# A conditioned transformer block on one core: GpSimd's place among VectorE's work, memory products in 32-row blocks, and where the last x load stands

## The chip, the cores and the metric

The kernel runs on one core of a Trainium2 chip. Its engines are TensorE (PE), VectorE (DVE), ScalarE (ACT), GpSimd (POOL) and SyncE (SP, which here only gives out transfers). Each engine runs its own list of instructions in order and waits on semaphores for the others. The metric is the device time of one execution in microseconds; the median of several runs counts.

## What is computed

One token block of 2048 rows and 448 features goes through a layer norm, an attention with a compressive memory, a second layer norm and a gated feed-forward layer. Shift, scale and gate vectors come from a condition `c`. Everything is bf16 outside.

```python
mod = silu(c) @ w_mod                        # sa, ca, ga, sb, cb, gb: six vectors of 448
h = layernorm(x) * (1 + ca) + sa
x = x + ga * A(h)
h = layernorm(x) * (1 + cb) + sb
x = x + gb * B(h)

# A: 16 heads of 28; 4 segments of 512 rows, M and z start at zero
phi = lambda t: where(t > 0, t + 1, exp(t))
for s in range(4):
    p = softmax(q_s k_s^T * scale + causal_mask)       # the causal mask stays within the segment
    a_mem = (phi(q_s) @ M) / (phi(q_s) . z + 1e-6)
    o_s = g * a_mem + (1 - g) * (p @ v_s)              # g = sigmoid(beta), one for each head
    M = M + phi(k_s)^T v_s ;  z = z + sum(phi(k_s))
A = concat(o_s) @ wo
# B
B = (sigmoid(h @ w_gate) * (h @ w_up)) @ w_down        # inner width 1792
```

## The kernel before

The 2048 rows are four segments of 512, each of four tiles of 128. The 16 heads are four groups of four; a head takes 32 partitions (`HP`), 28 of them data (`Dh`), so that one group fills 128. The column behind a head's 28 values of v is one, so that z comes as a column of M. All weights stay in SBUF after one load.

The code doesn't issue instructions directly. It builds a graph of nodes with `add`; a node names an engine (or several, of which the planner chooses one), a planned duration in ns, a function that writes its instructions, the nodes it depends on, the buffers it takes (`take`, `use`), and a priority. `Graph.run` (L207) then simulates the engines in time: whenever an engine is free it gives it the ready node with the highest rank plus priority. The numbers in `PRM` are those priorities, one for each node of a kind. On TensorE a change of `mode` costs `SWITCH` and staying gains `STAY`. A node with `lock=True` is a VectorE operation that the planner keeps apart from GpSimd's: in planned time a GpSimd node doesn't start before the last locked VectorE node has ended (`held`), and a locked VectorE node doesn't start while GpSimd is busy (`shut`). At the end (L287 to L289) the nodes' functions are called in planned order. Semaphores come afterwards from what the instructions read and write, in the order in which they were written out; each engine's list follows that order too. The planned times themselves leave nothing on the chip.

The order of stages: loads, layer norm and projections of segment 0 (`ln1`, `turned`, `proj`), then for every segment attention in two halves of two head groups (`attention`, `unit`), `memory` for the next segment, the output product and the second layer norm (`wo_ln2`), and `ffn`. The planner mixes all of this. Segments 0 and 1 turn normalised rows on TensorE (L745); the other layer norms turn them by transposing transfers on the Sync queue (L690).

What the change and the prediction touch:
- `load` (L422) puts one transfer on the Sync queue (`nc.sync`) or on ScalarE's; `load_x` (L458) loads tiles of x. L654 loads tiles 12 to 15; L655 loads the down weights in four pieces; L652 loads the gate weights through ScalarE's queue.
- `wz` (L494) is the last tile of `x_sb`, index 15, set to zero by VectorE at the start. ScalarE's fills (L511) read it, and so do the dummy products (L1058): 16 nodes of two products each, whose result nobody reads. Their priority is far below everything else, so that they fill TensorE's idle time in the plan.
- `W_p` (L641) copies the q and k weights into padded form; the projection products are L805 (q, k) and L817 (v).
- `memory` (L836): phi of k (L830 to L833), a transposing transfer (L841), four products of 128 x 128 for each head group (L847), an update of `M_sb` on VectorE (L854, L856), and a copy times the block mask `bmask` on VectorE or GpSimd (L860), which sets to zero what mixes different heads.
- `unit` (L930): the masked exponentials times v (L938), and for segments 1 to 3 phi of q times the masked memory in one full product (L949).
- GpSimd also does the layer norms' `rstd` (L559, L560), part of the causal masks (L910), of the weight scalings (L681) and of the modulations (L702).

Of the kernel before, what the change touches and what calls it, by code (L numbers as in the profile page):

```python
# [7 lines left out]
BF16 = mybir.dt.bfloat16  # L8
# [7 lines left out]
SWITCH = 96  # L16
# [29 lines left out]
    "mask": (1420295, 2300886, 1661567, 1988009, 1742158, 1915688, 1601937, 2188133, 1494944, 1748413, 1621429,  # L46
# [16 lines left out]
    "mem": (-214050, -174920, 501877, -265144, 92656, -155063, -11188, -639908, -57241, 71005, -88187, -198959, 48359,  # L63
# [68 lines left out]
class Graph:  # L132
# [74 lines left out]
    def run(self):  # L207
# [12 lines left out]
        while done < len(self.nodes):  # L220
            moved = False
            for e in ENGINES:
                if at[e] > t or (e == "POOL" and held > t):
                    continue
# [879 lines left out]
```

## Time and profile before

| | us |
|---|---|
| median of 3 runs | 297.54 |
| lowest and highest run | 293.26, 298.44 |
| the profiled execution | 292.1 |
| its span, first to last instruction | 290.4 |
| PE busy in the span | 245.0 (84%) |
| DVE busy | 203.7 (70%) |
| ACT busy | 152.8 (53%) |
| POOL busy | 62.4 (21%) |

An engine's busy time counts its instructions, not its waits. PEld is the load of weights into TensorE, which runs beside products. A row of a timeline merges instructions of one line that follow each other; the idle time before the first of them stands in brackets, with what ended it. PEclk is TensorE's granted clock as a share of 2.4 GHz, so 0.50 is the lower level, 1.2 GHz.

### The profile page before, as it was taken

Reading aid. Unit: us, or ns where it says so; the run is one execution under the profiler, and the core shown is the slowest. Engines: PE = TensorE matmul, PEld = TensorE weight load, DVE = VectorE, ACT = ScalarE, POOL = GpSimd, SP = SyncE. Lnnn points to the kernel's source line nnn. Section 1 sums busy time; section 2 is a strip of 40 time slices with the busy share of each in tenths; the row PEclk is TensorE's granted clock in tenths of the full one; section 3 lists DMA queues with packets and bytes.
Section 4 is the critical chain, followed back from the end, with each engine's and each line's share of the span. In section 5 each row is a group of like instructions: output and inputs, shape, how many; then the busy total and the mean of one; then the engine's idle time right before and its main releaser. Section 6 shows DMA issues by size and latency. Waiting matters only on the chain. (4 is left out here: it accounts for less than half of the span.)

```text
span 290.4 us, 5584 instructions
## 1 busy us (share of the span) xinstructions
PE 245.0 (84%) x2185; PEld 108.0 (37%) x2185; DVE 203.7 (70%) x472; ACT 152.8 (53%) x186; POOL 62.4 (21%) x119
## 2 busy tenths in 40 slices
PE   8800089987598696998899999998999999999995
PEld 3600033533233232344355433443444434443442
DVE  5490006999989998899974999996989944414331
ACT  4220008879678966786645867776752133213210
POOL 7021000322506705057500200351010400000000
PEclk9955579999689977799999999999999999999999
DMA  7999976414330332000550011013210043000001
GB/s 198 218 225 223 216 227 141 83 38 91 84 72 3 82 73 64 18 2 18 78 116 2 18 52 33 2 33 47 59 34 0 3 87 81 16 18 16 19 16 47
DMA packets 32102, 20.73 MB, mean 71 GB/s; under 512 B 20491, under 2 KB 30412, under 8 KB 32076
## 3 DMA queue, kind: packets, MB, share of 16 engines
q1 hardware_dynamic: 29868, 17.11, 26.9%
q10 hardware_dynamic: 2208, 3.27, 5.3%
q8 instruction: 17, 0.28, 0.4%
q14 instruction: 9, 0.07, 0.1%
HBM read 11.07 MB, written 1.84 MB: 44 GB/s over the span
## 5 line engine op out<-in xcount | busy, mean ns | idle before, releaser
L1023 PE MATMUL ps<-hT,wgu 64*128 64x512 bf16 x784 | 96.3, 383 | 3.8 <-DVE fT L1030 1.5
L1028 ACT ACTIVATE tt<-ps 128x512 f32<-128x512 f32 x56 | 33.4, 596 | 63.8 <-PE ps L1023 61.9
L897 ACT ACTIVATE pT<-ps 128x2048 bf16<-128x2048 f32 x32 | 60.1, 1878 | 9.7 <-PE ps L883 8.8
L1030 DVE SCALAR_TENSOR_TENSOR fT<-tt,ps 128x512 bf16<-128x512 f32 x56 | 38.0, 681 | 34.5 <-ACT tt L1028 34.5
L1023 PEld LDWEIGHTS <-wgu 64*128 64x128 bf16 x784 | 39.7, 95 | 52.9 <-issue 17.6
L1042 PE MATMUL ps<-wd_sb,fT 128*128 128x448 bf16 x224 | 46.8, 353 | 0.0
L910 POOL TENSOR_SCALAR_AFFINE_SELECT pT<-pT 128x512 bf16<-128x512 bf16 x24 | 15.9, 673 | 74.8 <-ACT pT L897 58.7
L1058 PE MATMUL ps<-x_sb 128*128 128x448 bf16 x32 | 10.3, 495 | 24.3 <-DMA x_sb<-in_A_x_dram 23.1
L805 PE MATMUL ps<-hT,wqk 64*128 64x512 bf16 x224 | 28.9, 395 | 1.0 <-ACT pT L897 1.0
L1042 PEld LDWEIGHTS <-fT 128*128 128x128 bf16 x224 | 20.4, 98 | 23.6 <-issue 7.0
L788 ACT CAST kT<-ps 128x512 bf16<-128x512 f32 x11 | 6.5, 587 | 29.6 <-PE ps L805 29.4
L552 DVE BATCH_NORM_STATS2 st<-x_sb 128x6 f32<-128x448 bf16 x32 | 19.5, 611 | 1.5 <-DMA x_sb<-in_A_x_dram 1.1
L790 DVE CAST kT<-ps 128x512 bf16<-128x512 f32 x5 | 3.4, 675 | 24.6 <-PE ps L805 24.6
L883 PE MATMUL ps<-qT,kT 28*128 28x512 bf16 (+3 forms) x256 | 17.0, 312 | 3.5 <-ACT pT L903 1.5
L805 PEld LDWEIGHTS <-wqk 64*128 64x128 bf16 x224 | 11.6, 98 | 15.8 <-issue 6.2
L913 DVE TENSOR_TENSOR pT<-pT,cmask 128x512 bf16<-128x512 bf16 x40 | 17.0, 450 | 0.5 <-ACT pT L897 0.5
L903 ACT ACTIVATE pT<-ps 128x2048 bf16<-128x2048 f32 x8 | 15.0, 1881 | 3.6 <-PE ps L883 3.6
L560 POOL TENSOR_TENSOR rs<-rs,mhalf 128x1 f32<-128x1 f32 (+1 forms) x26 | 15.9, 613 | 2.2
L1001 PE MATMUL ps<-wo_sb,oT 128*128 128x448 bf16 x64 | 13.6, 353 | 1.5 <-DVE kT L790 1.2
L817 PE MATMUL ps<-wvv,hT 64*128 64x448 bf16 x112 | 13.3, 365 | 1.7 <-DVE vt L790 1.5
L559 POOL TENSOR_SCALAR rs<-mv 128x1 f32<-128x1 f32 (+1 forms) x26 | 6.2, 238 | 39.7 <-DVE mv L553 36.9
L938 PE MATMUL ps<-pT,vt 128*32 128x512 bf16 (+3 forms) x256 | 12.7, 315 | 2.3 <-DVE pT L913 1.7
(96 smaller groups left out, 273.4 us busy)
## 6 DMA issues: line engine op xcount, KB each, us to landing
out_dram<-ot SPq DMA_DIRECT2D x16, 112.0 KB, 1.7
hT<-hT SPq DMA_DIRECT2D x6, 256.0 KB, 3.2
hT<-hT SPq DMA_DIRECT2D x6, 192.0 KB, 2.7
x_sb<-in_A_x_dram SPq DMA_DIRECT2D x2, 448.0 KB, 13.5
wgu<-in_B_w_up_dram SPq DMA_DIRECT2D x1, 896.0 KB, 11.2
wd_sb<-in_B_w_down_dram SPq DMA_DIRECT2D x2, 448.0 KB, 9.5
wgu<-in_B_w_gate_dram ACTq DMA_DIRECT2D x1, 896.0 KB, 7.3
fT<-in_w_mod_dram SPq DMA_DIRECT2D x2, 392.0 KB, 13.0
```

Source lines behind the costliest of these rows:

```text
L552: nc.vector.bn_stats(st_r[:, st.at, :], src)
L560: nc.gpsimd.tensor_tensor(r, r, mhalf[:, 0:w], ALU.pow)
L805: nc.tensor.matmul(pf(b), lhsT=w, rhs=piece(hT, i, half), start=(i == 0), stop=(i == NP - 1))
L883: nc.tensor.matmul(ps[:, lg.at + hs, o:o + nq], lhsT=kT_r[r, k.at, hcs[u], kb * P:(kb + 1) * P], rhs=qT_r[r, q.at, hcs[u], kb * P:L], star ...
L897: nc.scalar.activation(pT_r[:, pTs[units[0]].at, :, w0:w0 + L], ps_, AF.Exp, scale=scale)
L903: nc.scalar.activation(dst, ps_.rearrange("p h (u w) -> p u h w", u=2), AF.Exp, scale=scale)
L910: nc.gpsimd.affine_select(out=blk, in_=blk, compare_op=ALU.is_ge, fill=0.0, base=0, pattern=[[0, 4], [1, P]], channel_multiplier=-1)
L913: nc.vector.tensor_tensor(blk, blk, cmask[:].rearrange("p (o k) -> p o k", o=1).to_broadcast([P, 4, P]), ALU.mult)
L1023: nc.tensor.matmul(pf(b), lhsT=wgu[half * HR:(half + 1) * HR, chunk_of(i, half), fs], rhs=piece(hT, i, half), start=(i == 0), stop=(i == N ...
L1028: a = act(485, lambda gp=gp, tt=tt: nc.scalar.activation(tt_r[:, tt.at, :], pf(gp), AF.Tanh, scale=0.5), [n], use=[gp, tt], prio=pr("tanh" ...
L1030: f = dve(597, lambda up=up, tt=tt, ft=ft: nc.vector.scalar_tensor_tensor(fT_r[:, ft.at, :], tt_r[:, tt.at, :], 1.0, pf(up), op0=ALU.add, ...
L1042: nc.tensor.matmul(pf(b)[:, 0:D], lhsT=fT_r[:, fts[fc].at, t * P:(t + 1) * P], rhs=wd_sb[:, fc, :], start=(fc == 0), stop=(fc == NFC - 1))
```

## The change

Three things change in the code, and the planner's numbers with them.

- In the plan a GpSimd node may start no earlier than 175 ns (`BEHIND`) after the start of the last VectorE node. When the instructions are written out, the first instruction of each GpSimd node gets a semaphore wait on the last VectorE instruction whose planned end lies at or ahead of the GpSimd node's planned start.
- The memory is kept as blocks of 32 rows and 32 columns for each head, `M_sb` being 128 x 32 for a head group instead of 128 x 128. The update takes 16 small products for a head group, the read four small ones; `bmask` goes, a column `rmask` takes its place, and the copy runs on VectorE alone.
- The dummy products are defined ahead of the loads, and the load of tiles 12 to 15 depends on the last dummy and on ScalarE's fills.
- `SWITCH` is 164 ns from mode H to mode R and 96 for all other changes (96 for all before); `STAY`, `COST` and all numbers of `PRM` are new, so that the order of the nodes differs throughout.

```diff
-SWITCH = 96
+SWITCH = {("H", "R"): 164}
+OTHER = 96
+BEHIND = 175
...
-STAY = 25968
-COST = {"ACT": 0.86, "DVE": 1.009, "POOL": 0.81}
+STAY = 151782
+COST = {"ACT": 1.037, "DVE": 1.012, "POOL": 0.764}
...
-                if at[e] > t or (e == "POOL" and held > t):
+                if at[e] > t or (e == "POOL" and max(held, gate) > t):
...
-                    if e == "DVE" and n.lock:
-                        held = n.end
+                    if e == "DVE":
+                        gate = t + BEHIND
+                        if n.lock:
+                            held = n.end
...
+        block = tc.nc.cur_bb.bb.instructions
+        last = []
         for n in order:
-            if n.fn is not None:
-                n.fn(n.eng) if len(n.durs) > 1 else n.fn()
+            if n.fn is None:
+                continue
+            was = len(block)
+            n.fn(n.eng) if len(n.durs) > 1 else n.fn()
+            if n.eng == "DVE":
+                last.append((n.end, block[-1].name))
+            elif n.eng == "POOL":
+                before = [name for end, name in last if end <= n.start]
+                if before:
+                    tc.add_manual_dep(block[was], before[-1], mybir.DependencyInfo(
+                        mybir.DependencyClass.Sync, mybir.DependencyReason.DATA), reason="place among VectorE's work")
...
-    M_sb = const.tile([P, NHC, P], F32, name="M_sb")
+    M_sb = const.tile([P, NHC, HP], F32, name="M_sb")
...
-    rm_r = ring("rm", 5, [P, P], BF16)
+    rm_r = ring("rm", 5, [P, HP], BF16)
...
+    n_warm = None
+    for i in range(NWARM):
+        n_warm = add("PE", 740 if i < 7 else 380, warm_fn, [n_wz, n_warm], prio=-4 * BIG if i else 2 * BIG, mode="F", take=() if i else [b_w],
+            use=[b_w] if i else ())
...
-    load_x("SP", 3 * TPS, 4 * TPS, first(18), 41)
+    load_x("SP", 3 * TPS, 4 * TPS, first(18), 41, [n_warm, n_pads, *n_vpad, *n_vone, *n_opad])
...
         nc.vector.tensor_reduce(epsc[:], eps4[:], axis=mybir.AxisListType.X, op=ALU.add)
+        nc.vector.tensor_reduce(rmask[:], rsel[:], axis=mybir.AxisListType.X, op=ALU.add)
...
                 for kb in range(TPS):
-                    nc.tensor.matmul(pf(b)[:, 0:P], lhsT=pk_r[:, pk.at, kb, :],
-                                     rhs=vt_r[:, vt_of[s].at, kb, hc * 4:(hc + 1) * 4, :].rearrange("p h e -> p (h e)"),
-                                     start=(kb == 0), stop=(kb == TPS - 1))
+                    for hs in range(4):
+                        r = slice(hs * HP, (hs + 1) * HP)
+                        nc.tensor.matmul(pf(b)[r, 0:HP], lhsT=pk_r[:, pk.at, kb, r], rhs=vt_r[:, vt_of[s].at, kb, hc * 4 + hs, :],
+                                         start=(kb == 0), stop=(kb == TPS - 1), tile_position=(0, HP * hs),
+                                         skip_group_check=True)
...
-                    nc.vector.tensor_tensor(M_sb[:, hc, :], M_sb[:, hc, :], pf(b)[:, 0:P], ALU.add)
-            u = dve(197, up, [m, M_n.get((s, hc))], use=[b], prio=pr("mem", s))
+                    nc.vector.tensor_tensor(M_sb[:, hc, :], M_sb[:, hc, :], pf(b)[:, 0:HP], ALU.add)
+            u = dve(110, up, [m, M_n.get((s, hc))], use=[b], prio=pr("mem", s))
...
-            rm_n[(s + 1, hc)] = shared((200, 430), lambda e, hc=hc, rm=rm: vec(e).tensor_tensor(
-                rm_r[:, rm.at, :], M_sb[:, hc, :], bmask[:], ALU.mult), [u, n_masks], take=[rm], prio=pr("mem", s))
+            rm_n[(s + 1, hc)] = dve(110, lambda hc=hc, rm=rm: nc.vector.tensor_scalar(
+                rm_r[:, rm.at, :], M_sb[:, hc, :], rmask[:, 0:1], None, op0=ALU.mult), [u, n_coef], take=[rm],
+                prio=pr("mem", s), lock=True)
...
-            m = add("PE", 220, lambda: nc.tensor.matmul(pf(mem), lhsT=rm_r[:, rm.at, :], rhs=pq_r[:, pq.at, :],
-                                                        start=True, stop=True),
-                    [f, rm_n[(s, hc)]], take=[mem], use=[pq, rm], mode="F", prio=pr("phi", s))
+
+            def read():
+                for hs in range(4):
+                    r = slice(hs * HP, (hs + 1) * HP)
+                    nc.tensor.matmul(pf(mem)[r, :], lhsT=rm_r[r, rm.at, :], rhs=pq_r[r, pq.at, :], start=True, stop=True,
+                                     tile_position=(HP * hs, HP * hs), skip_group_check=True)
+            m = add("PE", 235, read, [f, rm_n[(s, hc)]], take=[mem], use=[pq, rm], mode="D", prio=pr("phi", s))
```

The masks' set-up on GpSimd loses `bmask` and gains one small selection for `rsel`; both kinds of edits that stand above as "..." follow from these.

## Rows read from the trace of the kernel before

**Rows 1.** The profile page: span and instructions.

```profile
span 290.4 us, 5584 instructions
```

**Rows 2.** Timeline, TensorE, 0 to 48: start, us, engine, line, operation, tiles, count, idle.

```profile
5.56 3.25 PE L1058 MATMUL ps<-x_sb 128*128 128x448 bf16 x14
...
11.44 3.06 PE L745 MATMUL ps<-ident,xn 128*128 128x128 bf16 x32
37.61 3.14 PE L1058 MATMUL ps<-x_sb 128*128 128x448 bf16 x8 [23.10 <-DMA x_sb<-in_A_x_dram]
40.68 3.63 PE L805 MATMUL ps<-hT,wqk 64*128 64x512 bf16 x32
```

**Rows 3.** The same timeline's VectorE and ScalarE, 0 to 52.

```profile
16.87 1.63 DVE L640 COPY wqk<-wd_sb 64x784 bf16<-64x784 bf16 x4
...
16.09 1.45 ACT L767 ACTIVATE hT<-ps,cols 128x512 bf16<-128x512 bf16 x2 [1.56 <-DVE hT L765]
...
44.69 0.60 ACTq L425 DMA_DIRECT2D wgu<-in_B_w_gate_dram  x1
```

**Rows 4.** The same timeline's Sync queue, 0 to 48 and 40 to 100.

```profile
24.47 0.55 SPq L425 DMA_DIRECT2D x_sb<-in_A_x_dram  x1
25.08 10.68 SPq L425 DMA_DIRECT2D wd_sb<-in_B_w_down_dram  x4
...
61.69 2.60 SPq L841 DMA_TRANSPOSE pk<-pq  x2
```

**Rows 5.** Windows: stretch, its us, busy us of each engine (instructions), clock, DMA.

```profile
14.50:37.60 23.10, 0.00 (x1) 0.00 (x0) 6.74 (x18) 1.48 (x3) 3.09 (x8) 0.50 1.09 229
...
50.00:150.00 100.00, 84.67 (x836) 36.35 (x830) 93.60 (x226) 77.22 (x89) 38.73 (x57) 0.91 0.30 60
150.00:210.00 60.00, 58.30 (x553) 26.32 (x550) 50.45 (x117) 42.41 (x45) 9.61 (x18) 1.00 0.16 32
210.00:290.40 80.40, 77.13 (x585) 33.32 (x581) 41.55 (x78) 20.91 (x33) 4.52 (x10) 1.00 0.11 30
```

**Rows 6.** DMA issues by line: tiles, queue, count, KB each, median us to landing.

```profile
wgu<-in_B_w_gate_dram ACTq DMA_DIRECT2D x1, 896.0 KB, 7.3
...
wd_sb<-in_B_w_down_dram SPq DMA_DIRECT2D x2, 448.0 KB, 9.5
...
pk<-pq SPq DMA_TRANSPOSE x12, 2.4
```

**Rows 7.** GpSimd and VectorE at 97, then lines (busy, mean) and lines (min/median/max).

```profile
97.27 3.07 POOL L681 TENSOR_TENSOR wd_sb<-wd_sb,rep 128x448 bf16<-128x448 bf16 x3
...
97.73 3.06 DVE L565 TENSOR_SCALAR xn<-x_sb,mv,rs 128x448 bf16<-128x448 bf16 x4
...
L565 DVE TENSOR_SCALAR xn<-x_sb,mv,rs 128x448 bf16<-128x448 bf16 x32 | 13.7, 465 | 0.5 <-POOL rs L560 0.5
...
L831 DVE TENSOR_SCALAR e<-qT 128x512 bf16<-128x512 bf16 x12 | 5.2, 435 | 0.0
...
L565 DVE TENSOR_SCALAR xn<-x_sb,mv,rs x32: 354/391/1100, 7.5 to 232.3; 128x448 bf16<-128x448 bf16 x32
L831 DVE TENSOR_SCALAR e<-qT x12: 260/286/1116, 87.3 to 206.6; 128x512 bf16<-128x512 bf16 x12
```

**Rows 8.** Small products (timeline, lines) and the memory's copies (lines).

```profile
68.50 0.40 PE L847 MATMUL ps<-vt,pk 128*128 128x128 bf16 x4
...
9.65 1.93 PE L604 MATMUL ps<-silu,pT 112*128 112x1 bf16 x62 [0.82 <-DMA pT<-in_w_mod_dram]
44.24 0.39 PE L883 MATMUL ps<-qT,kT 28*128 28x512 bf16 x4
...
L847 PE MATMUL ps<-vt,pk x48: 218/219/230, 68.5 to 174.3; 128*128 128x128 bf16 x48
...
L949 PE MATMUL ps<-pq,rm 128*128 128x512 bf16 x12 | 4.3, 402 | 0.5 <-DVE pq L833 0.5
L856 DVE TENSOR_TENSOR M_sb<-M_sb,ps 128x128 f32<-128x128 f32 x8 | 2.2, 277 | 1.4 <-PE ps L847 1.4
```

More of the change, by code (lines that the diff above doesn't have):

```diff
@@ L22 @@
 PRM = {
[23 rows of a table removed]
-    "mask": (1420295, 2300886, 1661567, 1988009, 1742158, 1915688, 1601937, 2188133, 1494944, 1748413, 1621429,
[16 rows of a table removed]
-    "mem": (-214050, -174920, 501877, -265144, 92656, -155063, -11188, -639908, -57241, 71005, -88187, -198959, 48359,
[22 rows of a table removed]
-    "tanh": (518834, 901538, 371356, 312956, 429296, 1610358, 1231833, 455336, 658639, 1233093, 953232, 1034923,
[16 rows of a table removed]
-    "phi": (92371, 88481, 47667, 108382, -497773, 32202, 492785, 282150, 660225, 55845, -9786, 163048, 345946, 155916,
[3 rows of a table removed]
-}
-STAY = 25968
-COST = {"ACT": 0.86, "DVE": 1.009, "POOL": 0.81}
[23 rows of a table added]
+    "mask": (1520615, 1413694, 1279386, 2003105, 1818148, 1973568, 1670422, 2469718, 1732752, 2449207, 2306151,
[16 rows of a table added]
+    "mem": (-185723, 115729, 59349, 101126, -27425, -125584, 150803, 226014, 77645, 95180, -386111, -12099, 159007,
[22 rows of a table added]
+    "tanh": (1916179, 1874612, 1112957, 1758741, 1844683, 2214238, 1662134, 1941088, 2051357, 2010608, 1710485,
[16 rows of a table added]
+    "phi": (177400, -21809, 241433, -242751, 352146, 109506, 5113, 407805, 377077, 37510, -3877, 641907, 208593,
[3 rows of a table added]
+}
+STAY = 151782
+COST = {"ACT": 1.037, "DVE": 1.012, "POOL": 0.764}
 class Slot:
@@ L205, in place, with run @@
         return got
-    def run(self):
+    def run(self, tc):
         self.ranks()
@@ L215, in run @@
         at = dict.fromkeys(ENGINES, 0.0)
-        held = 0.0
+        held = gate = 0.0
         mode = None
@@ L251, in run @@
                     if e == "PE":
-                        extra = SWITCH if n.mode != mode else 0
+                        extra = SWITCH.get((mode, n.mode), OTHER) if n.mode != mode else 0
                         mode = n.mode
@@ L279, in run @@
                 continue
-            times = [x for x in (*at.values(), held) if x > t]
+            times = [x for x in (*at.values(), held, gate) if x > t]
             times += [x for e in ENGINES for n in avail[e] if len(n.durs) > 1
@@ L375 @@
     coef = const.tile([P, NHC, 2], F32, name="coef")
-    bmask = const.tile([P, P], BF16, name="bmask")
+    rmask = const.tile([P, 1], F32, name="rmask")
     cmask = const.tile([P, P], BF16, name="cmask")
@@ L438, in vec @@
         return nc.vector if e == "DVE" else nc.gpsimd
-    def shared(durs, fn, deps=(), prio=0, **kw):
-        return add(("DVE", "POOL"), durs, fn, deps, prio=prio, lock=True, **kw)
     def pool_op(dur, fn, deps=(), prio=0, **kw):
@@ L522, in masks_fn @@
                                 pattern=[[1, P]], channel_multiplier=-1)
-        nc.gpsimd.memset(bmask[:], 1.0)
-        blk = bmask[:].rearrange("p (h e) -> p h e", e=HP)
-        nc.gpsimd.affine_select(out=blk, in_=blk, compare_op=ALU.is_ge, fill=0.0, base=0, channel_multiplier=1,
-                                pattern=[[-HP, 4], [0, HP]])
-        nc.gpsimd.affine_select(out=blk, in_=blk, compare_op=ALU.is_ge, fill=0.0, base=Dh - 1, channel_multiplier=-1,
-                                pattern=[[HP, 4], [0, HP]])
-    n_masks = pool_op(1500, masks_fn, prio=2 * BIG + 2e6)
+    n_masks = pool_op(500, masks_fn, prio=2 * BIG + 2e6)
     hsel = const.tile([P, 4], F32, name="hsel")
     eps4 = const.tile([P, 4], F32, name="eps4")
+    rsel = const.tile([P, 4], F32, name="rsel")
     def hsel_fn():
         nc.gpsimd.memset(hsel[:], 1.0)
-        for c0, mul in ((0, 1), (HP - 1, -1)):
-            nc.gpsimd.affine_select(out=hsel[:], in_=hsel[:], compare_op=ALU.is_ge, fill=0.0, base=c0,
-                                    pattern=[[-HP * mul, 4]], channel_multiplier=mul)
+        nc.gpsimd.affine_select(out=hsel[:], in_=hsel[:], compare_op=ALU.is_ge, fill=0.0, base=0,
+                                pattern=[[-HP, 4]], channel_multiplier=1)
+        for dst, last in ((rsel, Dh - 1), (hsel, HP - 1)):
+            nc.gpsimd.affine_select(out=dst[:], in_=hsel[:], compare_op=ALU.is_ge, fill=0.0, base=last,
+                                    pattern=[[HP, 4]], channel_multiplier=-1)
         nc.gpsimd.memset(eps4[:], 0.0)
@@ L540, in hsel_fn @@
                                 channel_multiplier=1, pattern=[[-HP, 4]])
-    n_hsel = pool_op(1130, hsel_fn, prio=2 * BIG + 1e6)
+    n_hsel = pool_op(1320, hsel_fn, prio=2 * BIG + 1e6)
     def layer_norms(srcs, deps, prio, hT=None, prev=None):
@@ L641, with warm_fn @@
             W_p.append(add(("DVE", "ACT", "POOL"), (415, 838, 830), pad, [W_qk[half], n_pads, n_th, *ln0], prio=BIG, lock=True))
+    b_w = bank()
+    def warm_fn():
+        for _ in range(2):
+            nc.tensor.matmul(pf(b_w)[:, 0:D], lhsT=wz[:, 0:P], rhs=wz, start=True, stop=True)
+    n_warm = None
+    for i in range(NWARM):
+        n_warm = add("PE", 740 if i < 7 else 380, warm_fn, [n_wz, n_warm], prio=-4 * BIG if i else 2 * BIG, mode="F", take=() if i else [b_w],
+            use=[b_w] if i else ())
     load_wm(2, 1, fT_flat[:, 2 * NK * D:], first(10), (17,))
@@ L671, in coef_fn @@
         nc.vector.tensor_reduce(epsc[:], eps4[:], axis=mybir.AxisListType.X, op=ALU.add)
-    n_coef = dve(900, coef_fn, [n_cf, n_hsel], lock=True)
+        nc.vector.tensor_reduce(rmask[:], rsel[:], axis=mybir.AxisListType.X, op=ALU.add)
+    n_coef = dve(1000, coef_fn, [n_cf, n_hsel], lock=True)
     ga_mm, n_ga = mod_rep(2, 0, 1.0)
@@ L846, in mm @@
                 for kb in range(TPS):
-                    nc.tensor.matmul(pf(b)[:, 0:P], lhsT=pk_r[:, pk.at, kb, :],
-                                     rhs=vt_r[:, vt_of[s].at, kb, hc * 4:(hc + 1) * 4, :].rearrange("p h e -> p (h e)"),
-                                     start=(kb == 0), stop=(kb == TPS - 1))
-            m = add("PE", 4 * 60, mm, [tr] + [v_n[(s, t)] for t in range(TPS)], take=[b], use=[pk, vt_of[s]], mode="F", prio=pr("mem", s))
+                    for hs in range(4):
[3 more added lines that the diff above has]
+                                         skip_group_check=True)
+            m = add("PE", 4 * 60, mm, [tr] + [v_n[(s, t)] for t in range(TPS)], take=[b], use=[pk, vt_of[s]], mode="C", prio=pr("mem", s))
             def up(hc=hc, b=b):
                 if s == 0:
-                    nc.vector.tensor_copy(M_sb[:, hc, :], pf(b)[:, 0:P])
+                    nc.vector.tensor_copy(M_sb[:, hc, :], pf(b)[:, 0:HP])
                 else:
-                    nc.vector.tensor_tensor(M_sb[:, hc, :], M_sb[:, hc, :], pf(b)[:, 0:P], ALU.add)
-            u = dve(197, up, [m, M_n.get((s, hc))], use=[b], prio=pr("mem", s))
+                    nc.vector.tensor_tensor(M_sb[:, hc, :], M_sb[:, hc, :], pf(b)[:, 0:HP], ALU.add)
+            u = dve(110, up, [m, M_n.get((s, hc))], use=[b], prio=pr("mem", s))
             M_n[(s + 1, hc)] = u
             rm = rm_of[(s + 1, hc)] = Slot("rm")
-            rm_n[(s + 1, hc)] = shared((200, 430), lambda e, hc=hc, rm=rm: vec(e).tensor_tensor(
-                rm_r[:, rm.at, :], M_sb[:, hc, :], bmask[:], ALU.mult), [u, n_masks], take=[rm], prio=pr("mem", s))
+            rm_n[(s + 1, hc)] = dve(110, lambda hc=hc, rm=rm: nc.vector.tensor_scalar(
+                rm_r[:, rm.at, :], M_sb[:, hc, :], rmask[:, 0:1], None, op0=ALU.mult), [u, n_coef], take=[rm],
+                prio=pr("mem", s), lock=True)
     def attention(s, hcs, oT, prev):
@@ L1052, in ffn @@
                 use=[ot], lag=2300)
-    b_w = bank()
-    def warm_fn():
-        for _ in range(2):
-            nc.tensor.matmul(pf(b_w)[:, 0:D], lhsT=wz[:, 0:P], rhs=wz, start=True, stop=True)
-    n = None
-    for i in range(NWARM):
-        n = add("PE", 740 if i < 7 else 380, warm_fn, [n_wz, n], prio=-4 * BIG if i else 2 * BIG, mode="F", take=() if i else [b_w],
-            use=[b_w] if i else ())
     for s in range(NSEG):
@@ L1072 @@
         ffn(s, *wo_ln2(s, oT, on))
-    G.run()
+    G.run(tc)
 _INS = ['A_x', 'A_wq', 'A_wk', 'A_wv', 'A_wo', 'A_beta', 'B_x', 'B_w_gate', 'B_w_up', 'B_w_down', 'c', 'w_mod']
```

160 rows, old and new, of the table PRM are left out of this document.

## Prediction

> **What bounds the kernel now.** I read the timeline of TensorE's first 48 us first, because the page's slices show a hole in TensorE's row there. TensorE turns the normalised rows of segment 0 (L745) until 14.50, and then does nothing until 37.61, when eight dummy products start; the row says that they waited 23.10 us for the transfer into x_sb. The first real projection (L805) starts at 40.68 [rows 2]. The dummy products read the last tile of x_sb, zeros that VectorE wrote at the start. In the order that the planner wrote out, the load of tiles 12 to 15 stands ahead of the last four dummy pieces (eight products), so these wait until the real x has come. Nothing else asks for that wait: the operands of the first projections are there by 18.5, when the last weight copy ends, and the last hT chunk is written at 17.54 [rows 3]. What waits for TensorE stands still with it, and in ScalarE's queue so do the gate weights' loads behind such work (44.69) [rows 3].
>
> The windows then show the rest. In the hole VectorE is busy 6.7 of 23.1 us. From 50 to 150 VectorE is busy 93.6 of 100 us and TensorE 84.7, at a mean granted clock of 0.91 (a mean over stretches at 2.4 GHz and some at 1.2); from 150 to 210 TensorE is busy 58.3 of 60, from 210 on 77.1 of 80.4 [rows 5]. So there are three stages: a hole, a middle where VectorE sets the pace, and a long TensorE-bound end. The chain of waits on the page covers only the last stage and says nothing about the first two.
>
> **Last x load behind the dummy products.** The load gets the 16 dummy pieces and ScalarE's fills as predecessors, so it is written out behind them, and the wait turns round: the transfer waits for the readers of the zeros. What is removed is bounded from below by the wait itself, 23.1 us. Counted to L805, it is more: the eight products may run at 14.50, and L805 then follows the last chunks of hT and not the dummies. If its first matmuls follow the chunks from about 16 on, all behind them moves by 40.68 - 16 = 24.7; if L805 starts only with the last chunk at 17.54, by 23.1. I take 24. At this point nothing of the load's own price is due: the Sync queue comes to this load at 24.47 [rows 4], long after the dummies' end (17.6 even at the slow 3.14 us of [rows 2]), so the queue doesn't wait.
>
> What is late next? The loads. In the hole they ran for nothing; now the work comes 24 us earlier and they don't. The hole moved 229 GB/s with the transfer engines full (share 1.09) [rows 5]. The Sync queue issues its last weight loads from 25.08 to 35.76 [rows 4], and TensorE's first products of the memory (L847), at 68.50 now [rows 8], move to 44.5. Their operand comes through transposing transfers on the Sync queue, issued at 61.69 now and due at 37.7 after the change [rows 4], behind all weight loads. And ScalarE's queue now gives out the gate loads (896 KB and a second, smaller one [rows 6]; 448 x 1792 values of two bytes, 1.6 MB) at about 44.69 - 24 = 20.7 instead of 44.69, into the same full engines: 1.6 MB at 229 GB/s is 7 us more for all that lands behind. Without them the Sync queue's loads end near 42.6 (an estimate: the last of the four issues that took 10.68 us [rows 4] starts near 33.1, and such a load takes 9.5 us to land [rows 6]), with them up to 49.6; a transpose behind, with its own 2.4 us [rows 6], lands at 45 to 52. So the first memory products wait between 0.5 and 7.5 us; I take 4. That the order of the last x load against the four down-weight loads can turn round (it may now stand behind them, some 5 to 10 us later, since the planner holds it until the dummies end) falls into the same bound. The Trainium skill's page "DMA: Bandwidth & Descriptors", section "Issuing engines are not separate DMA queues", speaks against the change's full gain here: loads from two engines end on the same 16 transfer engines and interleave. The full share in the hole agrees with it; by that rule the gate loads cost the 7 us, and were they on a path of their own the term would be nothing.
>
> **GpSimd waits for VectorE.** The planner keeps VectorE's locked operations and GpSimd's apart in its own time; the kernel before has no such order on the chip. The trace shows what it costs. While GpSimd's weight scalings ran (97.27, three of them), four normalisations on VectorE took 3.06 us together [rows 7]. Mean against median of two groups: L565 (465 - 391) x 32 = 2.4 us, L831 on qT (435 - 286) x 12 = 1.8, in all 4.2 us [rows 7]; five more locked groups (L831 on kT, L833, L913, L969, L982) show the same with smaller differences and are put at as much again, so I allow up to 9. GpSimd is busy 38.7 us between 50 and 150 and 14.1 later [rows 5], so most of it lies in the stage that VectorE paces, where a saved microsecond is nearly one of time. New is a wait on each GpSimd piece, with its signal from VectorE. The bound from below is nothing: GpSimd is idle for 61 of 100 us in the middle stage [rows 5]. From above: VectorE waits for GpSimd's rstd in the layer norms and TensorE for its masks, and I see 57 GpSimd instructions in the middle stage [rows 5], some 40 pieces (an rstd is two); at 0.1 us of each on the path that is 4 us. Only VectorE's work in the plan's past is awaited, which GpSimd was meant not to overtake, so I take 1 for it and 6 for the collisions: 5 saved together; bounds, 9 saved and 3 lost.
>
> **Memory as 32-row blocks.** Four products of 128 columns took 0.40 us together and 219 ns each [rows 8], so 0.06 us from one to the next and 0.24 for four on the array. Now there are 16 of 32 columns. The nearest row is that of 62 one-column products in 1.93 us, 31 ns each [rows 8]: 16 x 31 = 0.50, so 0.26 more for each of 12 groups, 3.1 us of TensorE. Since they use four column groups side by side they may cost less, down to nothing. Of this I take 1 on the path: the groups stand between 68.5 and 174.3 [rows 8], mostly in the middle, where TensorE is idle for 15 us. The Trainium skill's page "TensorEngine Tiling (Array Packing)", section "Instruction Overhead", speaks against this edit: a matmul pays about 60 cycles whatever its columns. At 2.4 GHz that is 25 ns, an estimate of 0.40 us for 16; by it the term is 1.9 us in all instead of 3.1. The row of 31 ns bears the rule out; I keep the row. The read of the memory becomes four 32-row products on tiles of their own; four logits products on 28-row tiles take 0.39 us together, one full product 0.40 [rows 8], so this costs nothing. On VectorE the update shrinks from 277 ns [rows 8] to something between that and half, and the masked copy goes wholly to VectorE, part of it having been on GpSimd: less and more cancel within 1 us. The mask that is no longer built, and one small reduction more, lie in the load phase.
>
> **The new planner weights** reorder everything. No row prices them. TensorE's idle time between 50 and 210 is 15.3 + 1.7 = 17 us [rows 5]; a better order can win part of that and no more, a worse one could lose as much. I take nothing, and keep the bounds with the collisions in the range.
>
> **The sum.** Of the profiled execution's 292.1 (span 290.4 [rows 1] and 1.7 around it): -24 hole, +4 loads, -5 GpSimd, +1 memory: 292.1 - 24 = 268.1 at its plainest. The part that I can't price leans one way, as the middle stage holds 17 us of idle time beside slow clock, and the new switch price and GpSimd gate bring plan and chip closer: I take 2 for it and say **266**. The profile stands 5.4 below the median of 297.54, so the after's median may lie above its own profile too; the sum leaves that out, and the range holds it.
>
> **Rivals.**
> *The hole closes, collisions go* (0.62): 266, its own range 254 to 273.
> *Collisions stay* (0.16): VectorE isn't made to wait for GpSimd, only the reverse, and a VectorE operation right behind the awaited one still meets it. For: VectorE's operations follow one another at once, as the four of [rows 7] do. Against: the plan leaves such a place free. Then 292.1 - 24 + 4 + 1 = 273.
> *The loads take the hole's place* (0.14): transposes behind all loads land at 52 against 44.5, 7.5 us of wait, and the rest doesn't hide it: 292.1 - 24 + 7.5 + 1 = 277, less 5 if the collisions go. For: the full engines; against: VectorE, which paces the middle, has other work.
> *The wait moves and doesn't vanish* (0.05): the planner puts the last dummies into a much later gap of TensorE, and the Sync queue stands with the x load before the transposes. At 10 us of standing 292.1 - 24 + 10 + 4 + 1 = 283. Against: the dummy products ahead of the turned rows are all but eight, and done by 8.81 [rows 2].
> *GpSimd's waits become the path* (0.03), the slower side: 85 GpSimd instructions from 50 on [rows 5], some 60 pieces; from 24/60 = 0.4 us of each on the path the gain is gone, and at 0.5 it is 292.1 - 24 + 30 = 298. Against: GpSimd's own idle time.
>
> Within 2% is about what a measurement of this kernel can tell from no change. Faster by over 2% hold all cases but the last and a part of the fourth: 0.95; same 0.03, slower 0.02. The range: low end all of the idle time between 50 and 210 won less what the loads take, 292.1 - 24 - 17 + 3 = 254; high end the three costs at their bounds, 7.5, 3.1 and 3, 292.1 - 24 + 13.6 = 282. Outside it 0.15 is left, the fourth and fifth cases and a plan much better.
>
> **What would show it.** The eight dummies right behind L745, no wait on x_sb before L1058, L805 at 16 to 18; gate loads on ScalarE's queue near 21; a wait of TensorE for pk at 44 to 52, if any; L565 and L831 with means near their medians; L847 in 16 products of about 30 ns. It is wrong if L805 starts later than 20, if the middle stage (to the end of VectorE's high share) takes longer than now, or if GpSimd's waits end VectorE's idle time.

## The result and the profile after

The changed kernel takes 273.23 us (median of 4 runs, 272.84 to 274.04), the kernel before 295.4 beside it; the ratio is 0.936, 95% interval 0.928 to 0.943. Medians here are over all runs; ratios and their intervals leave out the longer runs of a slower state that some executions of every kernel show. The profiled execution took 274.0 us with a span of 272.3, so the spans differ by 18.1 us.

TensorE's timeline after (start, us, engine, line, operation, tiles, count, idle before) is to be held against [rows 2] and the L847 row of [rows 8]. Line numbers are those of the changed kernel: L657 are the dummies, L765 the turned rows, L825 the projections of q and k, L869 the memory's products.

```profile
11.63 4.16 PE L765 MATMUL ps<-ident,xn 128*128 128x128 bf16 x32
15.58 2.45 PE L657 MATMUL ps<-x_sb 128*128 128x448 bf16 x6
17.96 6.24 PE L825 MATMUL ps<-hT,wqk 64*128 64x512 bf16 x56
...
53.35 0.30 PE L869 MATMUL ps<-vt,pk 128*32 128x32 bf16 x16 [6.88 <-DMA pk<-pq]
```

The hole is gone: six of the last eight dummies follow the turned rows at once (the last two run at 25.23), and the first projection starts at 17.96 instead of 40.68. In its place stands a wait of 6.88 us at 46.5, for a transposed operand of the memory. The Sync queue shows why (against [rows 4]):

```profile
25.07 14.65 SPq L441 DMA_DIRECT2D wd_sb<-in_B_w_down_dram  x4
40.20 3.80 SPq L441 DMA_DIRECT2D x_sb<-in_A_x_dram  x1
44.11 6.61 SPq L710 DMA_TRANSPOSE hT<-xn  x4
50.81 1.22 SPq L861 DMA_TRANSPOSE pk<-pq  x1
```

Four down-weight loads and then the last x load go out between 25 and 44, and only then the first transpose. Two marks on TensorE, the first q and k projection and the first memory product, cut the span into three:

| stretch | before | after | difference |
|---|---|---|---|
| start to the first projection | 40.68 | 17.96 | -22.7 |
| from there to the first memory product | 27.82 | 35.39 | +7.6 |
| from there to the end | 221.9 | 218.95 | -2.9 |

Of the 7.6 us more between the two marks, 6.1 are idle time of TensorE (7.6 against 1.5 before). The rest is its busy time, 27.8 us against 26.3, at a mean granted clock of 0.89 against 1.00.

Behind the first memory product, a window up to the start of the last logits products holds nearly the same work in both kernels, before and then after (as [rows 5]: busy us of PE, PEld, DVE, ACT and POOL, clock, DMA share, GB/s):

```profile
68.50:209.35 140.85, 125.31 (x1154) 53.84 (x1147) 125.84 (x287) 103.44 (x111) 43.98 (x70) 0.94 0.23 47
53.35:193.53 140.18, 126.41 (x1353) 54.21 (x1355) 121.19 (x310) 104.49 (x115) 32.61 (x59) 0.93 0.24 47
```

VectorE is busy 4.7 us less there, and the window itself is shorter by 0.7 only. VectorE was relieved and the time hardly followed. The groups by line (busy, mean ns of one, idle before) tell of the collisions and of the memory; they are to be held against [rows 7, 8]:

```profile
L575 DVE TENSOR_SCALAR xn<-x_sb,mv,rs 128x448 bf16<-128x448 bf16 x32 | 11.4, 400 | 1.5 <-POOL rs L570 1.5
L851 DVE TENSOR_SCALAR e<-qT 128x512 bf16<-128x512 bf16 x12 | 3.4, 279 | 0.0
L976 PE MATMUL ps<-pq,rm 32*32 32x512 bf16 x48 | 4.6, 383 | 1.4 <-DVE fT L1057 1.1 <-DVE pq L853 0.2
L869 PE MATMUL ps<-vt,pk 128*32 128x32 bf16 x192 | 3.4, 184 | 8.4 <-DMA pk<-pq 7.8 <-ACT aT L808 0.4 <-DVE fT L1057 0.2
L882 DVE TENSOR_SCALAR rm<-M_sb,rmask 128x32 bf16<-128x32 f32 x12 | 2.9, 245 | 0.2
L878 DVE TENSOR_TENSOR M_sb<-M_sb,ps 128x32 f32<-128x32 f32 x8 | 1.2, 162 | 0.0
```

The normalisations take 400 ns on average instead of 465, the phi step on q 279 instead of 435: the stretched ones are gone. Over all VectorE operations that lasted more than 80 ns beyond the median of their kind, what they lasted beyond it (the operations' stretch below) sums to 0.5 us; before it was 10.1.

### The profile page after: what moved, and what is told of

Read it like the earlier page. It is cut to its first block, busy times and chain, and to the rows that moved or that the text cites. A ratio compares the mean times of both kernels' runs of the same rounds, so it can differ in the third digit from the quotient of the medians.

```text
span 272.3 us, 5953 instructions
## 1 busy us (share of the span) xinstructions
PE 244.9 (90%) x2365; PEld 110.9 (41%) x2365; DVE 194.0 (71%) x484; ACT 152.0 (56%) x188; POOL 48.9 (18%) x104
## 5 line engine op out<-in xcount | busy, mean ns | idle before, releaser
L1050 PE MATMUL ps<-hT,wgu 64*128 64x512 bf16 x784 | 94.5, 385 | 2.3 <-DVE aT L810 0.9
L1069 PE MATMUL ps<-wd_sb,fT 128*128 128x448 bf16 x224 | 45.8, 353 | 0.2 <-DVE kT L810 0.2
L933 POOL TENSOR_SCALAR_AFFINE_SELECT pT<-pT 128x512 bf16<-128x512 bf16 x29 | 18.1, 635 | 73.1 <-DVE O L1009 21.1
L825 PE MATMUL ps<-hT,wqk 64*128 64x512 bf16 x224 | 28.8, 392 | 0.4 <-DVE x_sb L1031 0.4
L825 PEld LDWEIGHTS <-wqk 64*128 64x128 bf16 x224 | 12.5, 97 | 14.0 <-issue 3.0
L1076 DVE TENSOR_TENSOR ot<-ps,x_sb 128x448 bf16<-128x448 f32 x16 | 9.8, 614 | 9.0 <-PE ps L1069 8.7
L837 PE MATMUL ps<-wvv,hT 64*128 64x448 bf16 x112 | 14.7, 397 | 0.6 <-DMA hT<-hT 0.5
L936 DVE TENSOR_TENSOR pT<-pT,cmask 128x512 bf16<-128x512 bf16 x35 | 14.1, 425 | 1.3 <-ACT pT L920 1.3
L722 DVE TENSOR_SCALAR hT<-hT,cols 128x512 bf16<-128x512 bf16 (+1 forms) x19 | 6.5, 402 | 11.4 <-DMA hT<-xn 11.4
L961 PE MATMUL ps<-pT,vt 128*32 128x512 bf16 (+3 forms) x256 | 11.9, 304 | 1.7 <-DVE pT L936 1.1
L575 DVE TENSOR_SCALAR xn<-x_sb,mv,rs 128x448 bf16<-128x448 bf16 x32 | 11.4, 400 | 1.5 <-POOL rs L570 1.5
```

Source lines behind the costliest of these rows:

```text
L825: nc.tensor.matmul(pf(b), lhsT=w, rhs=piece(hT, i, half), start=(i == 0), stop=(i == NP - 1))
L933: nc.gpsimd.affine_select(out=blk, in_=blk, compare_op=ALU.is_ge, fill=0.0, base=0, pattern=[[0, 4], [1, P]], channel_multiplier=-1)
L1050: nc.tensor.matmul(pf(b), lhsT=wgu[half * HR:(half + 1) * HR, chunk_of(i, half), fs], rhs=piece(hT, i, half), start=(i == 0), stop=(i == N ...
L1069: nc.tensor.matmul(pf(b)[:, 0:D], lhsT=fT_r[:, fts[fc].at, t * P:(t + 1) * P], rhs=wd_sb[:, fc, :], start=(fc == 0), stop=(fc == NFC - 1))
```

## The experiments

Four kernels at a time ran on one chip, with the kernel before beside them; a median stands with its ratio to that and the ratio's interval. The changed kernel itself, run again beside the late loads below, gave 272.93 (0.923, 0.914 to 0.933).

**The hole alone.** In the kernel before, one line:

```diff
-    wz = x_sb[:, NSEG * TPS - 1, :]
+    wz = rep[:, 1, :]
```

> The kernel before with one line changed: the zeros that the dummy products and ScalarE's fills read lie in the still unused second half of rep, no longer in x_sb. The written order of all instructions is that of the kernel before, only the wait for the last x load is gone. Theory (hole and loads): the first projections start at 17 to 18 instead of 40.68, TensorE's first memory products wait 5 to 8 us for their transposed operand behind the weight loads, collisions stay at some 10 us of VectorE; profiled time 292.1 - 22.7 + 7 = 276. Rival (the wait for the loads in the changed kernel comes from the x load's new place behind the down weights, or from the new order): those products wait under 2 us here, and the time is 268 to 271.

Measured: 272.99 us (0.928, 0.921 to 0.934), as fast as the whole change, and between the theory's 276 and the rival's 268 to 271. TensorE's timeline of this kernel, and two of its lines (mean ns):

```profile
15.29 0.72 PE L805 MATMUL ps<-hT,wqk 64*128 64x512 bf16 x3 [0.28 <-DVE wqk L640]
...
50.28 0.40 PE L847 MATMUL ps<-vt,pk 128*128 128x128 bf16 x4 [1.34 <-DMA pk<-pq]
...
54.74 0.40 PE L847 MATMUL ps<-vt,pk 128*128 128x128 bf16 x4 [2.75 <-DMA pk<-pq]
```

```profile
L565 DVE TENSOR_SCALAR xn<-x_sb,mv,rs 128x448 bf16<-128x448 bf16 x32 | 13.7, 464 | 0.5 <-POOL rs L560 0.5
...
L831 DVE TENSOR_SCALAR e<-qT 128x512 bf16<-128x512 bf16 x12 | 5.2, 436 | 0.0
```

The first projection comes at 15.29, the first memory product 34.99 us later, against 27.82 with the hole and 35.39 in the changed kernel. So the way between these two marks grows by the same 7 us in the old order, with the x load still ahead of the down weights. Its make-up differs: the wait for transposed operands comes in pieces, two of them in the lines above, and is 5.5 us on TensorE's products in all (7.8 in the changed kernel, 1.3 in the kernel before), while TensorE's busy time up to the first memory product is 3.8 us longer than before, at a mean granted clock of 0.90. The collisions stay at their full size. The rival, that the new order or the x load's new place made this wait, falls for most of it.

**The waits of GpSimd, in the old order.** The same kernel, and the changed kernel's `add_manual_dep` loop at the end of `run`.

> The same kernel (zeros in rep, order of before) with the changed kernel's waits of GpSimd on VectorE, taken from the old plan's times. Theory (the waits pay for themselves by the collisions): L565 and L831 near their medians, 4 to 6 us less than the kernel with the zeros alone, about 271. Rival (what the changed kernel won behind its first memory products comes from the new order): no gain, 275 to 277, since the old plan leaves no 175 ns for the signal; or a loss of 1 to 3 us, if the waits themselves are on the path.

Measured: 267.98 us (0.910, 0.903 to 0.917), 5.0 less than without the waits, on the same chip. The lines:

```profile
L576 DVE TENSOR_SCALAR xn<-x_sb,mv,rs 128x448 bf16<-128x448 bf16 x32 | 11.3, 389 | 0.6 <-POOL rs L571 0.6
...
L842 DVE TENSOR_SCALAR e<-qT 128x512 bf16<-128x512 bf16 x12 | 3.6, 302 | 0.0
```

Both groups are back near their medians (391 and 286), and the operations' stretch, summed as above, falls from 8.8 to 2.1 us. 6.7 us less of VectorE brought 5.0 of time, with intervals clear of each other. That agrees with the theory's gain of 4 to 6; the rivals fall.

**The waits, taken out of the changed kernel.** Order unchanged:

```diff
-                before = [name for end, name in last if end <= n.start]
+                before = []
```

> The changed kernel without the waits of GpSimd on VectorE; the order of all instructions is the same. Theory (collisions): stretched VectorE operations come back, 6 to 10 us of VectorE in all instead of 0.5, and the time rises from 273 to 277 to 279. Rival (VectorE's stretch is hidden where TensorE paces): 273 to 274. Rival (the waits lie on the path): 269 to 272.

Measured: 273.33 us (0.926, 0.919 to 0.933). With the waits the changed kernel has 273.23 and 272.93 on other chips (0.936 and 0.923), and 272.68 (0.925) on this chip in the form with full products, below. The theory missed; the time is that of the first rival:

```profile
L575 DVE TENSOR_SCALAR xn<-x_sb,mv,rs 128x448 bf16<-128x448 bf16 x32 | 12.7, 441 | 1.4 <-POOL rs L570 1.3
...
L851 DVE TENSOR_SCALAR e<-qT 128x512 bf16<-128x512 bf16 x12 | 3.8, 314 | 0.0
```

The operations' stretch comes back, but as 5.1 us instead of 8.8; this order puts 12 of 14 down-weight scalings on VectorE where the old one had 12 of 14 on GpSimd, which leaves less to collide. The time doesn't rise measurably. The same waits are worth 5 us in one order and nothing in the other.

That need not mean that the 5.1 us are hidden, as the rival has it. Without the waits the first projection starts at 15.90, and 256.2 us follow; with them it starts at 17.96 and 17.21 in the changed kernel's two profiles, and 254.3 and 252.5 follow. So the waits seem to lose 1.3 to 2.1 us ahead of the first projection and to win 1.9 to 3.7 behind it. These are single profiles, and no run separates the two.

**The memory in full products again**, in the changed kernel:

```diff
-                    for hs in range(4):
-                        r = slice(hs * HP, (hs + 1) * HP)
-                        nc.tensor.matmul(pf(b)[r, 0:HP], lhsT=pk_r[:, pk.at, kb, r], rhs=vt_r[:, vt_of[s].at, kb, hc * 4 + hs, :],
...
+                    nc.tensor.matmul(pf(b)[:, 0:P], lhsT=pk_r[:, pk.at, kb, :],
...
-                rm_r[:, rm.at, :], M_sb[:, hc, :], rmask[:, 0:1], None, op0=ALU.mult)
+                rm_r[:, rm.at, :], M_sb[:, hc, :], bmask[:], ALU.mult)
...
-                for hs in range(4):
-                    r = slice(hs * HP, (hs + 1) * HP)
-                    nc.tensor.matmul(pf(mem)[r, :], lhsT=rm_r[r, rm.at, :], rhs=pq_r[r, pq.at, :], start=True, stop=True,
...
+                nc.tensor.matmul(pf(mem), lhsT=rm_r[:, rm.at, :], rhs=pq_r[:, pq.at, :], start=True, stop=True)
```

> The changed kernel with the memory as full 128 x 128 products again (four for an update, one for a read), the block mask and VectorE's copies over 128 columns; planned order and waits as in the changed kernel. Theory from the changed kernel's trace (16 small products took 0.30 us against 0.40 for four full ones, VectorE's copy 0.18 against 0.27 and the masked copy 0.25 against 0.3): the full form is 0 to 2 us slower, 273 to 275. Rival, the prediction's own term (31 ns for each small product, 3.1 us more TensorE in the block form): the full form is 1 to 3 us faster, 270 to 272.

Measured: 272.68 us (0.925, 0.918 to 0.931), no difference. Its lines, against L976, L869, L882 and L878 above:

```profile
L874 PE MATMUL ps<-vt,pk 128*128 128x128 bf16 x48 | 5.4, 243 | 7.7 <-DMA pk<-pq 7.0 <-ACT aT L815 0.4 <-DVE fT L1059 0.3
L979 PE MATMUL ps<-pq,rm 128*128 128x512 bf16 x12 | 4.7, 405 | 2.2 <-DVE fT L1059 1.9 <-DVE pq L860 0.4
L887 DVE TENSOR_TENSOR rm<-M_sb,bmask 128x128 bf16<-128x128 f32 x12 | 3.5, 291 | 0.2
L883 DVE TENSOR_TENSOR M_sb<-M_sb,ps 128x128 f32<-128x128 f32 x8 | 2.0, 262 | 0.0
```

The blocks are cheaper in each line, 3.4 us against 5.4 for the products and 1.4 us less of VectorE in the two lines shown, and none of it shows in the time.

**The queue ahead of the transposes.** In the changed kernel the four down-weight loads are written out behind the memory's third transpose; the plan is untouched. The moved nodes are taken out of `order` and put back ahead of the first node of their engine with a later planned start:

```diff
+        if eng == "SP" and land >= 45:
+            n.late = 45000
...
+        for n in [n for n in order if hasattr(n, "late")]:
+            order.remove(n)
+            i = next(i for i, o in enumerate(order) if o.eng == n.eng and o.fn is not None and o.start >= n.late)
+            order.insert(i, n)
```

> The changed kernel unchanged, as the measure for the three that run with it: 273, with TensorE waiting some 7 us for the first memory products' operand at 46 to 53.

> The changed kernel with one move in the written order: the four loads of the down weights stand on the Sync queue behind the third transposing transfer for the memory, instead of ahead of the last x load and of all transposes. The plan and every other place are the same. Theory (the transposes wait in the queue behind 1.6 MB): the last x load goes out near 25, the transposes near 38 to 42, TensorE's wait for the first memory products falls from 6.9 us to under 2, the time from 273 to 266 to 268. Rival (VectorE paces this stretch and has other work lined up behind): the wait comes back elsewhere, 271 to 273.

Measured: 268.31 us (0.908, 0.901 to 0.916), 4.6 less than the changed kernel beside it, 4.4 by the ratios, whose intervals just touch. The Sync queue of the changed kernel as run here, then that with the late loads, and the first memory products of both:

```profile
39.52 3.44 SPq L441 DMA_DIRECT2D x_sb<-in_A_x_dram  x1
43.06 6.45 SPq L710 DMA_TRANSPOSE hT<-xn  x4
49.60 2.53 SPq L861 DMA_TRANSPOSE pk<-pq  x2
...
52.16 0.30 PE L869 MATMUL ps<-vt,pk 128*32 128x32 bf16 x16 [5.78 <-DMA pk<-pq]
```

```profile
24.61 0.40 SPq L445 DMA_DIRECT2D x_sb<-in_A_x_dram  x1
38.67 6.17 SPq L716 DMA_TRANSPOSE hT<-xn  x4
44.94 2.53 SPq L867 DMA_TRANSPOSE pk<-pq  x2
...
52.87 2.19 SPq L445 DMA_DIRECT2D wd_sb<-in_B_w_down_dram  x4
...
47.47 0.28 PE L875 MATMUL ps<-vt,pk 128*32 128x32 bf16 x16 [0.41 <-DMA pk<-pq]
```

The first transpose goes out 4.4 us earlier, the first memory product starts 4.7 us earlier, and its wait falls from 5.78 to 0.41. So the loads in the Sync queue were the cause of the wait. In front of the transposes the queue now stands empty from 25 on, and they wait for VectorE's rows: the first goes out at 38.67, and the normalised rows that these transposes turn are written from 38.26 on. How much of the wait counts in time is less sure than the 4.6 us: the two profiles differ by 3.0 us, and 0.9 of it lies ahead of the first projection.

**The gate loads.** Instead of the down weights, the two loads on ScalarE's queue were moved behind the first memory products, by the same code with `eng == "ACT" and land >= 34`; and then both.

> The changed kernel with the two gate-weight loads on ScalarE's queue moved to planned time 45 us, behind the first memory products, instead of 19 us; the Sync queue's order is unchanged. Theory (both queues share the transfer engines, so 1.6 MB less land ahead of the transposes): the Sync queue gets through its loads 5 to 7 us earlier, TensorE's wait falls from 6.9 to 0 to 2 us, the time to 267 to 269. Rival (the Sync queue's own loads set its pace and the gate loads ran beside them): the Sync queue's issues end at 44 as before and the time stays at 272 to 273.

> Both moves together. Theory (one wait, removed once): as good as the better of the two single moves, 265 to 268, not the sum. Rival (each move removes a wait of its own): 260 to 264. Rival (the late loads then arrive too late for the weight scalings on VectorE or for the feed-forward products): above 270.

Measured: 271.14 us (0.921, 0.911 to 0.931) for the gate loads and 272.31 (0.916, 0.904 to 0.928) for both. With the gate loads late:

```profile
24.54 11.44 SPq L445 DMA_DIRECT2D wd_sb<-in_B_w_down_dram  x4
36.09 2.69 SPq L445 DMA_DIRECT2D x_sb<-in_A_x_dram  x1
38.88 6.76 SPq L716 DMA_TRANSPOSE hT<-xn  x4
...
48.23 0.28 PE L875 MATMUL ps<-vt,pk 128*32 128x32 bf16 x16 [2.48 <-DMA pk<-pq]
...
PE ps L875 <- DMA pk<-pq: 7.8, 4, 3.8
```

The Sync queue gives its loads out 4.2 us sooner (38.78 against 42.96 where the x load's issue ends), so the gate loads on the other queue did hold it up, but not for the full 7 us that the bytes alone would make. The Trainium skill's page "DMA: Bandwidth & Descriptors", section "Issuing engines are not separate DMA queues", says that transfers of several engines run on the same 16 and interleave; this agrees in kind. The first memory products wait less, but the last row (us in total, times, the longest) shows that the wait comes back at later ones: 7.8 us in all, against 6.5 in the changed kernel beside it.

With both late the longest wait of VectorE for a transfer is one for the down weights (total, times, longest):

```profile
DVE wd_sb L709 <- DMA wd_sb<-in_B_w_down_dram: 6.1, 1, 6.1
```

With the down weights alone late VectorE has no such wait. That is the pair's second rival, loads that come too late for the weight scalings, though it is read from the longest of the four runs (274.19). Neither run's time is clearly below the changed kernel's. On the time the two runs are inconclusive: nothing is added up, and the down weights' own gain is not seen again.

**Order or blocks, and the x load's place.** First, in the old order, zeros in `rep`, waits and the memory in blocks, that is the change without the new numbers and without the x load's new place (half of the memory's masked copies stay on GpSimd). Second, the changed kernel with its x load written out ahead of the down weights, its zeros in `rep`, so that the load needn't wait for the dummies:

```diff
-    wz = x_sb[:, NSEG * TPS - 1, :]
+    wz = rep[:, 1, :]
...
+        n = next(n for n in order if hasattr(n, "early"))
+        order.remove(n)
+        order.insert(next(i for i, o in enumerate(order) if hasattr(o, "down")), n)
```

> Zeros in rep, the waits of GpSimd on VectorE and the memory in 32-row blocks, all in the order of the kernel before (its planner numbers): everything of the change but the new numbers and the x load's new place. Theory (blocks are worth nothing, the new order costs some 5 us): 267 to 269, as the kernel with zeros and waits alone. Rival (the blocks cost what the order seems to cost, by their changes of tile mode on TensorE): 271 to 274.

> The changed kernel, its zeros in rep, and the last x load written out just ahead of the four down-weight loads instead of behind them; all else in the same order. Theory (the queue in front of the transposes is as long either way; the load's place only decides when x arrives): TensorE's wait for the first memory products stays at 5 to 7 us, 272 to 274. Rival (the x load's new place is what costs the changed kernel its 5 us): 267 to 269.

Measured on one chip, 6 runs each: 268.34 us (0.916, 0.911 to 0.921) and 273.50 us (0.928, 0.920 to 0.935). The x load's place is free:

```profile
24.00 0.62 SPq L444 DMA_DIRECT2D x_sb<-in_A_x_dram  x1
24.68 19.01 SPq L444 DMA_DIRECT2D wd_sb<-in_B_w_down_dram  x4
43.79 6.46 SPq L717 DMA_TRANSPOSE hT<-xn  x4
```

The queue reaches its first transpose at 43.79 with the x load in front and at 44.11 with it behind. What is left between 268.3 and 273.5 is the order that comes out of the new numbers (with it `SWITCH`, `STAY`, `COST` and the 175 ns): 1.2% of the time before by the ratios, some 3.5 us, the two intervals just touching.

The four kernels that ran together above show the same more clearly, and more (ratio to the kernel before):

| | without GpSimd's waits | with them |
|---|---|---|
| old order, zeros in `rep` | 0.928 | 0.910 |
| new order | 0.926 | 0.925 (memory in full products) |

With the waits the new order costs 1.5%, some 4.3 us, with intervals apart (0.903 to 0.917, 0.918 to 0.931). Without the waits it costs nothing. So the order's loss and the waits' missing gain are one and the same; they must not be counted twice. The clearest differences in the traces: from the first projection to the first logits the new order takes 6.2 us (24.14 - 17.96), the old 4.2 (19.94 - 15.73), so ScalarE's exponentials start some 5 us later (25.4 against 20.6); and the last logits stand at 191.1 in the changed kernel's second profile, at 184.9 in the old order's. At the end of the spans 3.0 of these 6 us are left. In the new order with the waits the first projection starts at 16.3 to 18.0 (seven profiles), in the old order with them at 14.7 to 15.7 (four). Which of the order's choices costs this was not tested.

**Toward a faster version.** The old order with zeros in `rep` and waits, and the down-weight loads late by the code above (planned time 47.9 us), all four and the last two of them:

> Zeros in rep and waits, old order, and the four down-weight loads moved on the Sync queue behind the first moves of segment 2's hT (planned time 47.9 us). Theory (the queue's wait is worth here what it was in the changed kernel, 4 to 5 us of 7): first memory products near 45, time 263 to 265. Rival (in the old order VectorE's first weight scaling needs the down weights early, so the wait only changes its place): 267 to 270.

> The same with only the last two of the four down-weight loads moved (672 KB of 1.6 MB); the first two, which the first scalings read, stay. Theory: by 229 GB/s some 2.9 us less ahead of the transposes, without the risk for the scalings: 265 to 267. Rival: 268, if 3 us of the wait are taken up by VectorE.

Measured: 267.22 us (0.913, 0.907 to 0.918) and 267.07 us (0.909, 0.902 to 0.915). With all four late, VectorE waits in their place:

```profile
DVE wd_sb L698 <- DMA wd_sb<-in_B_w_down_dram: 4.0, 1, 4.0
```

The first memory products come at 46.96 and 47.58 instead of 49.82, but the gain of the changed kernel isn't repeated: at most 1 us, inside the scatter. The old order scales its first down weights early and so takes the rival's side; the half move comes out between its theory and its rival. Both versions are some 2% faster than the changed kernel with its x load early beside them, and not clearly faster than zeros and waits alone.

## Why the prediction came out as it did

The direction was right, and the time lies in the range: 266 with 254 to 282 was said, 273.2 measured. It lies just outside the 254 to 273 of the case that got 0.62, and that case's mechanism didn't come in full, so the hit owes something to luck. In spans 26 us less were forecast and 18.1 came; of the 8 us between, 1.3 lie in the hole, 3.6 between the first projection and the first memory product, and 3.1 in all that follows (-6 taken for GpSimd, memory and order together, -2.9 measured).

- **Hole: 24 taken, 22.7 measured** to the first projection, below the lower bound of 23.1. The dummies and turned rows ran slower than I had put them: the 32 turned rows took 4.16 us instead of 3.06, at a mean granted clock of 0.62 between 10 and 15. In the old order it is 25.4 (40.68 - 15.29). The hole alone, with what the loads give back, is worth what the whole change is worth.
- **Loads: 4 taken, a wait of 6.9 measured**, near the upper bound of 7.5. The mechanism was right as written: the transposes stand behind the loads, the gate loads come early (at 23.90) and stretch the queue's issues (four down weights in 14.65 us instead of 10.68). I had taken the middle of 0.5 to 7.5. Of time, 4.4 to 4.6 us come back in this order where the down weights go out late, and at most 1 in the old one. The sum had no term for TensorE's lower clock in this stretch (0.89 instead of 1.00), which is 1.5 us of busy time. The full share in the hole says little for the page that I cited: only the Sync queue's loads were going out then, and the run with late gate loads is what bears on it. The x load did go behind the down weights, as the text allowed; that cost nothing.
- **GpSimd: 5 saved.** In the old order this is exact (5.0), and the collisions' size (up to 9, measured 8.8 and 10.1) nearly so. In the new order the same waits save nothing, so the term was priced on an order that the change replaces. That is the step that failed: the saving isn't a property of the wait alone.
- **Memory: 1 lost taken, nothing measured.** Its working was wrong: not 31 ns for each product, but 16 in 0.30 us where four full ones took 0.40. The step from one-column products on the whole array to products side by side in four column groups doesn't hold. The Trainium skill's page "TensorEngine Tiling (Array Packing)" says under "Instruction Overhead" that each matmul pays some 60 cycles, 25 ns at 2.4 GHz. The estimate from it, if each column group pays for itself, is three products behind the first at 25 ns and 0.18 us for one product: 0.26 us, near the rows of 0.27 to 0.30.
- **New numbers: 2 gained taken.** I leaned on the plan being closer to the chip; no row had said so. Without the waits the new order neither gains nor costs, with them it costs some 4 us. That is the same loss as the missing 5 of the waits: the two terms together were to bring 7 and brought nothing.

One sign of being wrong came: from the first projection to the last logits the changed kernel takes 175.6 us (193.53 - 17.96), the kernel before 168.7 (209.35 - 40.68). All of that lies ahead of the first memory product. VectorE's idle time, the other sign, ends on GpSimd for only 1.5 us in all.

The rivals: "the hole closes, collisions go" describes the trace, its time doesn't; 273 is the number given for "collisions stay", which is not what happened. "The loads take the hole's place" was worked out as 277, less 5 if the collisions go, so 272: its mechanism is the one that came, at a chance of 0.14. Its number isn't proof of it, since the runs don't show the 5 us in this order.

## What to carry to other kernels

A buffer that serves as a source of zeros early and as a load's target later ties the two by the order in which they are written out, and a filler product can so wait for a transfer that nobody needs yet; look for waits of work whose result is unused, and give the zeros a home that is written late. When a stall at the start goes, price the loads next: what ran for nothing during the stall now stands in the queue ahead of the first short transfers. A wait that keeps two engines apart is worth what the present order makes collide, less what it delays; measure it again after the order changes, and measure the order with and without it. Two parts of a change that each look like 5 us can be the same 5 us.

## What the runs showed that was not expected

Sixteen products of 128 x 32 in four column groups follow each other at about 8 ns on average ((0.30 - 0.18) / 15), against 29 ns for one-column products on the whole array ((1.93 - 0.16) / 61, 0.16 us being one product). In the trace they start in sets of four, one for each column group: some 10 ns pass within a set and mostly 25 from one set to the next.

And the granted clock of the same early instructions differs. In the seven profiles of the new order with the waits it is 0.58 to 0.82 between 10 and 15 us, in the one without them 1.00. From 5 to 10 TensorE was busy for 3.48 us in the changed kernel and for all 5.00 without the waits, and the first projection started at 17.96 and 15.90. The old order with the waits has 1.00 in three profiles and 0.66 in one, so the waits alone don't decide it.
